# Later places for output stores in the SP queue, and one weight slice instead of two, in a fused attention and expert kernel

## The chip, the cores and the metric

The kernel runs on one core of one Trainium2 chip. The metric is the device time of one execution in microseconds. Three runs of the kernel before took 211.05, 211.3 and 212.31 us; the median is 211.3 us.

A core has five engines that run side by side, each with a queue of its own that it works off in order: TensorE (PE; weight loads are shown apart as PEld), VectorE (DVE), ScalarE (ACT), GpSimd (POOL) and SyncE (SP). They wait for one another by semaphores. Transfers are issued by an engine's queue (here SP and POOL, once ACT) and carried out by 16 DMA engines.

## The reference

A block-wise linear attention with a decay per head, whose output goes through two matrix products with a quadratic gate between them:

```python
def _attn_ref(q, k, v, lam):                  # (4, 8, 768, 64): batch, head, position, feature
    Dmask = np.where(rel >= 0, lam ** rel, 0.0)
    for b in range(nb):                        # blocks of 64 positions
        intra = np.einsum('bhic,bhjc->bhij', qb, kb) * Dmask[None]
        intra = np.einsum('bhij,bhjd->bhid', intra, vb)
        inter = np.einsum('bhid,bhde->bhie', qb * lam_pow[None], kv_state)
        out[:, :, sl] = intra + inter
        kv_state = lam_block * kv_state + np.einsum('bhsd,bhse->bhde', kb * rev_pow, vb)

def _moe_ref(x, w_in, w_out):                  # x (3072, 512), w_in (512, 2048), w_out (2048, 512)
    h = x @ w_in
    g = np.where(h >= 1, h, np.where(h <= -1, 0.0, (h + 1) ** 2 / 4))
    return g @ w_out
```

Between them the attention output is laid out as x: 4 x 768 = 3072 tokens of 8 x 64 = 512 features. Inputs and output are float32; the kernel multiplies in bfloat16.

## The kernel before, in words

**Tiling.** The 3072 tokens are cut into 24 chunks of 128 positions, six to a batch (`NCB`). The first four chunks (`NU`) are handled by a special start with units `("e", u)`. Four chunks make a stage `s` of 512 tokens for the expert part; there are six stages.

**One chunk of attention.** SP loads k, q and v of a chunk, 256 KB each (`f_load`, L426). GpSimd multiplies k and q by the decay factors and casts them to bfloat16 (L450, L453; for the first chunks VectorE casts k), and ACT casts v (L443). From chunk 6 (`XT`) a DMA transpose issued by SP (`f_tx`, L470) brings q and k into the layout for TensorE; chunks 4 and 5 are transposed on TensorE (`f_t`, L461). Then TensorE makes a "visit" `("o", c)`: the scores of the next chunk (L492, or L556 in the first chunks), the products of masked scores with v (L527, L575), the part that comes from the state (L511, L571) and the k-v products for the state two chunks ahead (L500). So a visit needs the v cast of chunk c + 2. VectorE masks the scores and sums the state, ACT copies the results into `xT`.

**The expert part.** `("l1", n)` is a group of matmuls with w_in (L606) whose result ACT passes through a ReLU (L614) and VectorE through three steps (L622, L625, L630) into `gT`. `("l2", n)` is a group of four matmuls with w_out (L639); four such groups fill one output tile `py`, which ACT copies to `osb` (L664, eight buffers, `OB`) and SP stores (`f_out`, L673, or L671 with two transfers for the tiles of the first stage). The last tile is cut in two (L649, L656, L660).

**Weights.** w_in and w_out are loaded by GpSimd's queue in ten slices (`WSL`, L146; `load_w`, L152 and L153), cast from float32 to bfloat16 on the way. An entry (0, lo, hi) is a range of blocks of 128 columns of w_in, an entry (1, lo, hi) a range of blocks of 128 rows of w_out. Three tables tie them to other work by their number in the list: the first slice waits for a load of the start (`GATE_W`, L713), slices 2 and 3 stand behind two casts of the start on GpSimd (`AFTER_W`, L714), and the load of chunk 4's k, the first of the main part, waits for slice 7 to land (`GL`, L715).

**Order of the work.** No order is written out by hand. Each piece is entered with `add(key, engine, duration, function, needs, due, ...)`, and `run_plan` (L174) works through an assumed timeline: at each step it takes the engine that comes free first and, of its ready pieces, the one with the earliest due time. The order found so is the order of the instructions in each engine's queue, and the chip keeps it whatever the real times are. `slack` is a time by which a piece is held back in the plan after its needs are met; `dma` is the assumed time of a transfer. A store `("st", y)` has due -1, so the plan puts it ahead of other ready work of SP as soon as its copy `("y", y)` is done. Stores of the first stage wait in the plan for a visit as well.

Of the kernel before, what the change touches and what calls it, by code (L numbers as in the profile page):

```python
# [23 lines left out]
def kernel(  # L24
# [19 lines left out]
    NCB = S // C  # L44
# [8 lines left out]
    NCH = n_tok // C  # L53
    CPS = MS // C
# [68 lines left out]
    for t, base in ((mask2, 0), (mask2b, 128)):  # L123
# [19 lines left out]
    w_out_sb = big.tile([128, FO, d_model], BF16)  # L143
    w_in_r = moe_w_in.rearrange("(ko ki) n -> ki ko n", ki=128)
    w_out_r = moe_w_out.rearrange("(ko ki) n -> ki ko n", ki=128)
    WSL = [(0, 0, 2), (0, 2, 4), (0, 4, 6), (0, 6, 8), (0, 8, 12), (0, 12, 16),  # L146
           (1, 0, 4), (1, 4, 8), (1, 8, 12), (1, 12, 16)]

    def load_w(i):
# [19 lines left out]
    def add(key, eng, ns, fn, needs=(), due=None, extra=0, dma=0, perf=False, mode=("full", "full"), ring=1, slack=0, late=0):  # L169
        OPS[key] = Op(key, eng, ns, fn, list(needs), due, extra, dma, perf, mode, ring, slack)  # L170
        OPS[key].late = late
        ops.append(OPS[key])
# [104 lines left out]
    def mm(*cols):  # L277
        return sum(c / 2.4 + 3 for c in cols)
# [4 lines left out]
    kq, st = {}, {}  # L283
# [382 lines left out]
    def f_out(s, ms):  # L666
        m0 = s * MS + ms * 128
        if s == 0:

            for j in range(2):  # L670
                nc.sync.dma_start(out=out[m0:m0 + 128, :].rearrange("(p j) n -> j p n", j=2)[j], in_=osb[s, ms][HD[j], :])  # L671
        else:
            nc.sync.dma_start(out=out[m0:m0 + 128, :], in_=osb[s, ms])  # L673
# [41 lines left out]
    GL = {(NU, 1): 7}  # L715
    LDMA, TSP, TDMA = 1350, 2000, 1300
    Y_TO = 9
    XSLACK, LATE, LSTEP = 400, 3000, 400


    def eng_of(name):
# [13 lines left out]
            pos_, last_ld = pos_ + 1, ("ld", c, x)  # L735
    for i in range(len(WSL)):
        add(("w", i), "POOL", 900, lambda i=i: f_w(i), [AFTER_W.get(i), ("w", i - 1) if i else None, ("ld",) + GATE_W[i] if i in GATE_W else None],
            due=i * 1e-3, dma=2650 if WSL[i][2] - WSL[i][1] == 4 else 1650)

    for u in range(NU):  # L740
        sc, r = divmod(u, 2)
# [32 lines left out]
    for c in range(NU, NCH):  # L774
        od, cb = o_due(c), c % NCB
        for x in (1, 0):
            e = "DVE" if c < XT and x == 1 else "POOL"
            add(("cast", c, x), e, 605 if e == "DVE" else 1040,
                lambda c=c, x=x, e=e: cast(c, x, eng_of(e)),
                [("ld", c, x), prev_q(c, 1, "cast") + (x,), prev_q(c, NQK, "t") + ((x,) if c - NQK < NU else ()), prev_q(c, NQK, "o") if c - NQK < NCB else ("o", c - NQK - 2), ("qT", c - NQK)], extra=90)  # L780
        add(("cast", c, 2), "ACT", 530, lambda c=c: cast(c, 2, nc.scalar),
            [("ld", c, 2), prev_q(c, NVS, "o"), prev_q(c, 1, "cast") + (2,)], extra=95)
        if c < XT:
            add(("t", c), "PE", mm(*[128] * 8), lambda c=c: f_t(c),
                [("cast", c, 0), ("cast", c, 1), ("m", c - 1, 0) if c > NU else None, ("qT", "e", NU - 1), ("kT", "e", NU - 1)],
                due=od - 6000, extra=FILL)
            add(("kT", c), "DVE", 335, lambda c=c: f_tc(c, 1), [("t", c)], extra=95)
            add(("qT", c), "DVE", 335, lambda c=c: f_tc(c, 0), [("t", c)], extra=95)
        else:
            add(("qT", c), "SP", TSP, lambda c=c: f_tx(c), [("cast", c, 0), ("cast", c, 1), prev_q(c, NQT, "o")],  # L790
                due=-2, dma=TDMA, ring=1, slack=XSLACK, late=min(LATE, LSTEP * (c - XT)))
        if c == NCB:
            add(("s", c), "PE", mm(*[64] * 12), lambda c=c: f_ahead(c),
                [("kT", c), ("qT", c), ("fc", c), ("cast", c + 1, 1), ("cast", c + 1, 2), ("f", c, 0), ("f", c, 1), ("x", c - 1), ("o", c - 1)], due=od - 3000, extra=FILL, mode=T64)
        elif c < MG:
            add(("s", c), "PE", mm(*[128] * 4), lambda c=c: f_s(c),
                [("kT", c), ("qT", c), prev_q(c, 1, "m") + (0,), prev_q(c, 1, "m") + (1,)], due=od - 3000, extra=FILL, mode=T64)
        for par in range(2):
            add(("m", c, par), "DVE", 605 if c < NCB else 340, lambda c=c, par=par: f_m(c, par),
                [("s", c) if c < MG or c == NCB else ("o", c - 1), prev_q(c, 3, "o"), ("m", c, 0) if par else ("diag",) if c == NCB else None], extra=85)  # L800
        if c < NCB:
            add(("o", c), "PE", SWITCH + mm(*[128] * 8) + (mm(*[64] * 4) if cb < NCB - 1 else 0) + (mm(*[64] * 4) if c + 1 == NCB else 0),
                lambda c=c: f_visit(c),
                [("cast", c + 1, 1), ("cast", c + 1, 2)] * (c + 1 == NCB)
                + [("m", c, 0), ("m", c, 1), ("cast", c, 2), ("cast", c, 1), ("x", c - 1), ("o", c - 1), ("kT", c), ("qT", c)]
                + ([("st", "e", NU, 0), ("st", "e", NU + 1, 0)] if c == NU else [("ub", c - 1)]),
                due=od, extra=FILL, mode=("t64", "t128"))
            if cb < NCB - 1:
                add(("ub", c), "ACT", 270, lambda c=c: f_ub(c), [("o", c)], extra=100)
            add(("x", c), "ACT", 485, lambda c=c: f_x(c), [("o", c), ("x", c - 1)], extra=105)  # L810
            continue
        for a in range(1 if cb == NCB - 1 else 2):
            add(("f", c, a), "DVE", 340, lambda c=c, a=a: f_st(c, a),
                [("s", c - 1) if c == NCB + 1 else ("o", c - 1 if c == NCB else c - 2), ("m", c - 1, 1), ("f", c, 0) if a else None if cb == 0 else ("f", c - 1, 1), ("fc", c - 2)], extra=85)
        add(("fc", c), "ACT", 485 if cb < NCB - 1 else 270, lambda c=c: f_sc(c), [("f", c, 1), ("f", c, 0), ("o", c - NUB + 1)], extra=100)
        nx = c + 1 < NCH
        add(("o", c), "PE", mm(*[64] * (6 if cb else 5)) + (mm(*[64] * 10) if nx else 0),
            lambda c=c: f_visit2(c),
            [("kT", c + 1), ("qT", c + 1), ("cast", c + 2, 1), ("cast", c + 2, 2), ("fc", c + 1), ("fc", c), ("f", c + 1, 1), ("f", c + 1, 0)] * nx
            + [("m", c, 0), ("m", c, 1), ("fc", c), ("x", c - 1), ("o", c - 1), ("s", c)] + ([("fc", c - 1)] if cb else []),  # L820
            due=od, extra=FILL, mode=("t64", "t64"))
        add(("xa", c), "ACT", 270, lambda c=c: f_xh(c, 0), [("o", c), ("x", c - 1), ("l1", (c // CPS - 2) * FO - 1)], extra=105)
        add(("x", c), "ACT", 270, lambda c=c: f_xh(c, 1), [("xa", c), ("o", c), ("x", c - 1), ("l1", (c // CPS - 2) * FO - 1)], extra=105)
# [27 lines left out]
    for n2, (_, s, ms, kg) in enumerate(l2_order):  # L851
        n = PARTS.get(s, 1)
        if s == 0:
            need = [("g", W0.index((kg, ms // 2)))]
        else:
            need = [("g", (s * FO + (ms * n // CPS) * FO // n + (4 * kg + 4) // n - 1) // RW)]
        y = s * CPS + ms
        if y == NCH - 1:
            if kg == 0:
                for part, n in ((0, CUT), (1, d_model - CUT)):  # L860
                    add(("last", part), "PE", mm(*[n] * FO), lambda part=part: f_last(part),
                        [("g", n1 // RW), ("l2", n2 - 1), ("last", 0) if part else None, ("y", y - 2 + part)],
                        due=l_due[2, s, ms, kg] + part, extra=FILL)
                    add(("y", y + part), "ACT", 400 - 240 * part, lambda part=part: f_ylast(part),
                        [("last", part), ("y", y - 1 + part), ("st", y - OB)], extra=95)
                    add(("st", y + part), "SP", 550 if s else 1100, lambda part=part: f_stlast(part), [("y", y + part), ("st", y - 1 + part)], due=-1,
                        dma=300, ring=0.2)
            continue
        need += ([("x", "e", NU - 1, 0), ("x", "e", NU - 1, 1)] + bank[True][-2:]) if y < 2 else []
        add(("l2", n2), "PE", mm(*[512] * 4), lambda a=(s, ms, kg): f_l2(*a),  # L870
            need + [w_of(1, 4 * kg), ("l2", n2 - 1), ("y", y - 2) if kg == 0 else None], due=l_due[2, s, ms, kg], extra=FILL)
        if kg == 3:
            add(("y", y), "ACT", 490, lambda a=(s, ms): f_y(*a), [("l2", n2), ("y", y - 1), ("st", y - OB)], extra=95)
            add(("st", y), "SP", 550, lambda a=(s, ms): f_out(*a), [("y", y), ("o", 9 + y)] if s == 0 else [("y", y), ("st", y - 1) if y > CPS else None], due=-1, dma=650, ring=0.2)

    run_plan({"PE": 5000, "ACT": 5000, "DVE": 5000, "POOL": 5000, "SP": 800})

# [29 lines left out]
```

## Time and profile before

| what | value |
|---|---|
| median of three runs | 211.3 us |
| profiled execution, its time | 209.96 us |
| profiled execution, its span | 208.3 us |
| instructions in the span | 6084 |
| TensorE busy | 196.9 us (95%) |
| VectorE, ACT, GpSimd busy | 130.9, 119.9, 59.1 us |
| moved by DMA | 34.47 MB, mean 166 GB/s |
| weight slices of 256 KB: number, issue to landing | 4, median 5.8 us |
| weight slices of 512 KB of w_in, of w_out | 2, 9.3 us; 4, 14.9 us |

The span runs from the first to the last instruction of the profiled execution; its time holds 1.7 us more around it. All other numbers of a profile belong to that one execution. Busy time of PE is that of matmuls, which are pipelined. L12 is line 12 of the kernel; an arrow `<-` after an idle time names what ended it. Sizes of transfers are those of the bfloat16 side.

### The profile page before, as it was taken

The numbers are of one execution on the slowest core, as the hardware profiler recorded it, in microseconds if no ns is written. First come the engines' busy times: TensorE is split into PE (matmuls) and PEld (weight loads), VectorE is DVE, ScalarE is ACT, GpSimd is POOL, SyncE is SP. The second block draws the span as 40 slices with busy tenths as digits, with TensorE's granted clock in tenths as the row PEclk, the third lists the DMA queues.
The fourth block names the chain that finished last, engine by engine and source line by source line (L and its number), as shares of the span: only waits on it lengthen the run. The fifth ranks groups of instructions, "written<-read, shape, count | busy, mean of one in ns | idle before, by whom it ended". The sixth has DMA issues, their size and how long they took to land.

```text
span 208.3 us, 6084 instructions
## 1 busy us (share of the span) xinstructions
PE 196.9 (95%) x2599; PEld 123.3 (59%) x2626; DVE 130.9 (63%) x245; ACT 119.9 (58%) x225; POOL 59.1 (28%) x72
## 2 busy tenths in 40 slices
PE   7669999999999999999999999979999999999994
PEld 2457876447966866767777777544444444444443
DVE  1475886364795983597898867942599965454000
ACT  3565773226866764875775776553788655553121
POOL 5599300135343243313344322444210000000000
PEclk9999999999999999999999999999999999999999
DMA  4999999999999999999999999999961001101212
GB/s 115 293 246 157 184 207 207 217 223 205 157 203 232 217 211 233 209 221 227 213 213 237 196 147 218 184 183 259 199 148 50 3 0 50 50 3 50 101 50 101
DMA packets 96858, 34.47 MB, mean 166 GB/s; under 512 B 82368, under 2 KB 93888, under 8 KB 96832
## 3 DMA queue, kind: packets, MB, share of 16 engines
q1 hardware_dynamic: 91408, 29.89, 71.5%
q0 software_dynamic: 5280, 4.19, 13.5%
q8 instruction: 20, 0.33, 0.7%
q14 instruction: 6, 0.05, 0.1%
q10 hardware_dynamic: 144, 0.00, 0.0%
HBM read 27.27 MB, written 6.29 MB: 161 GB/s over the span
## 4 chain that ended last, share of the span: by engine, by line
PE 73%; DMA 13%; SPq 5%; POOL 5%; issue 1%; ACT 1%; ACTq 0%
PE py L639 33%; PE ph L606 32%; DMA w_out_sb<-in_moe_w_out_dram 9%; DMA x0f<-in_q_dram 3%; SPq L470 2%; POOL w_in_sb L152 2%; SPq L302 2%; DMA x2f<-in_v_dram 2%; PE py L649 2%; PE ps L500 1%; POOL w_out_sb L153 1%; POOL qs L315 1%; PE ps L492 1%; PE po L527 1%; PE pu L527 1%
## 5 line engine op out<-in xcount | busy, mean ns | idle before, releaser
L606 PE MATMUL ph<-xT,w_in_sb 128*128 128x256 bf16 (+2 forms) x740 | 90.5, 272 | 0.2
L639 PE MATMUL py<-w_out_sb,gT 128*128 128x512 bf16 x347 | 84.5, 379 | 2.4 <-issue 1.1
L614 ACT ACTIVATE r<-ph,one 128x512 bf16<-128x512 f32 x93 | 63.4, 687 | 32.6 <-PE ph L606 28.6
L606 PEld LDWEIGHTS <-w_in_sb 128*128 128x128 bf16 x768 | 63.8, 98 | 24.1
L639 PEld LDWEIGHTS <-gT 128*128 128x128 bf16 x368 | 34.8, 98 | 37.0 <-issue 1.1
L622 DVE TENSOR_SCALAR t<-r 128x1024 bf16<-128x1024 bf16 x48 | 21.8, 454 | 27.8 <-ACT r L614 27.6
L453 POOL TENSOR_TENSOR kq<-x1f,tkd 128x512 bf16<-128x512 f32 x18 | 19.7, 1095 | 61.4 <-DMA x1f<-in_k_dram 47.8
L630 DVE TENSOR_TENSOR gT<-w,t 128x1024 bf16<-128x1024 bf16 x48 | 35.8, 745 | 1.5
L625 DVE TENSOR_TENSOR w<-r,t 128x1024 bf16<-128x1024 bf16 x48 | 33.9, 707 | 1.5
L664 ACT COPY osb<-py 128x512 f32<-128x512 f32 x23 | 13.5, 586 | 21.7 <-PE py L639 17.6
L453 POOL TENSOR_TENSOR kq<-x0f,tqd 128x512 bf16<-128x512 f32 x18 | 19.9, 1106 | 5.8 <-DMA x0f<-in_q_dram 5.7
L565 DVE TENSOR_TENSOR sd<-ps,diag 128x256 bf16<-128x256 f32 x36 | 13.6, 418 | 11.0 <-PE ps L500 10.6
L443 ACT CAST vs<-x2f 128x512 bf16<-128x512 f32 x20 | 12.3, 615 | 9.2 <-DMA x2f<-in_v_dram 8.5
L544 ACT CAST us<-st 128x512 bf16<-128x512 f32 (+1 forms) x18 | 10.4, 578 | 6.3 <-DVE st L539 6.1
L539 DVE TENSOR_TENSOR st<-st,ps 128x256 f32<-128x256 f32 x30 | 12.5, 415 | 0.6
L548 ACT CAST xT<-po 128x256 bf16<-128x256 f32 x18 | 6.8, 378 | 3.1 <-PE pu L511 2.5
L450 POOL TENSOR_TENSOR kq<-x0f,tqd 128x512 bf16<-128x512 f32 x2 | 2.1, 1040 | 20.5 <-DMA x0f<-in_q_dram 20.5
L527 PEld LDWEIGHTS <-vs 64*64 64x64 bf16 x288 | 3.7, 107 | 6.3 <-issue 5.9
L500 PE MATMUL ps<-vs,kq 64*64 64x64 bf16 x264 | 6.1, 196 | 0.9 <-ACT vs L443 0.9
L548 ACT CAST xT<-pu 128x256 bf16<-128x256 f32 x18 | 6.8, 375 | 0.3 <-PE po L511 0.3
L381 DVE TENSOR_TENSOR sc<-ps,mask 128x512 bf16<-128x512 f32 x8 | 5.2, 681 | 2.1 <-PE ps L373 2.1
L275 PE MATMUL ph<-zz 128*128 128x512 bf16 (+1 forms) x16 | 4.9, 470 | 1.3 <-DVE one L108 1.3
(87 smaller groups left out, 123.9 us busy)
## 6 DMA issues: line engine op xcount, KB each, us to landing
x0f<-in_q_dram SPq DMA_DIRECT2D x24, 256.0 KB, 5.5
x1f<-in_k_dram SPq DMA_DIRECT2D x24, 256.0 KB, 5.1
x2f<-in_v_dram SPq DMA_DIRECT2D x24, 256.0 KB, 4.6
out_dram<-osb SPq DMA_DIRECT2D x19, 256.0 KB, 2.8
w_out_sb<-in_moe_w_out_dram POOLq DMA_DIRECT2D x4, 512.0 KB, 14.9
w_in_sb<-in_moe_w_in_dram POOLq DMA_DIRECT2D x4, 256.0 KB, 5.8
w_in_sb<-in_moe_w_in_dram POOLq DMA_DIRECT2D x2, 512.0 KB, 9.3
out_dram<-osb SPq DMA_DIRECT2D x8, 128.0 KB, 4.2
```

Of the source, the lines that this page charges most:

```text
L443: (nc.scalar.copy if eng is nc.scalar else eng.tensor_copy)(t, qkv_ld[c, x])
L453: eng.tensor_tensor(t.rearrange("p (i g) d -> p g i d", g=2), qkv_ld[c, x].rearrange(h4, g=2), tb.rearrange(h4, g=2), op=AX.mult)
L539: nc.vector.tensor_tensor(st[c][:, a], st[c][:, 0] if a else st[c - 1][:, 1], kv[c][a], op=AX.add)
L548: nc.scalar.copy(out=get_xT(s)[:, :, off:off + 64], in_=po_of(c, a))
L565: nc.vector.tensor_tensor(sc_sb[c][:, par], pst[c, par], _bc(diag, 1, HP), op=AX.mult)
L606: nc.tensor.matmul(ph[:, j * m:(j + 1) * m], lhsT=w_in_sb[:, ko, (ni + j) * 128:(ni + j + 1) * 128], rhs=xT[s][:, ko, part * m:(part + 1) ...
L614: nc.scalar.activation(out=r_t[grp][:, i, :], in_=ph_t[s, ni, part], func=AF.Relu, bias=one[:, 0:1])
L622: nc.vector.tensor_scalar(t_t[grp], r, 0.5, 1.0, op0=AX.mult, op1=AX.min)
L625: nc.vector.tensor_tensor(w_t[grp], r, t_t[grp], op=AX.subtract)
L630: nc.vector.tensor_tensor(gT[s][:, f - RW * n:f, part * m:(part + 1) * m], w_t[grp].rearrange("p a (b m) -> p (a b) m", m=m), t_t[grp].rea ...
L639: nc.tensor.matmul(py_t[s, ms], lhsT=gT[s][:, ko, ms * 128:(ms + 1) * 128], rhs=w_out_sb[:, ko, :], start=(ko == 0), stop=(ko == FO - 1))
L664: nc.scalar.copy(out=osb[s, ms], in_=py_t[s, ms])
```

## The change

Four edits. The third and fourth slice of w_in become one of 512 KB, so that nine slices are left, and all later numbers in the list go down by one, while the three tables keep their numbers. Each store except those of the last stage's four tiles gets a `slack` of 3000 in the plan, which moves it back in SP's queue. The plan's assumed time of a narrow slice goes from 1650 to 1800. And a visit of the first batch that also makes the next chunk's scores is entered in the plan with the time of these matmuls and with that chunk's transposed tiles among its needs; the condition is `MG <= c + 1 < NCB`, and both constants are 6 here.

```diff
-    WSL = [(0, 0, 2), (0, 2, 4), (0, 4, 6), (0, 6, 8), (0, 8, 12), (0, 12, 16),
+    WSL = [(0, 0, 2), (0, 2, 4), (0, 4, 8), (0, 8, 12), (0, 12, 16),
            (1, 0, 4), (1, 4, 8), (1, 8, 12), (1, 12, 16)]
...
-    XSLACK, LATE, LSTEP = 400, 3000, 400
+    XSLACK, LATE, LSTEP, OSLACK = 400, 3000, 400, 3000
...
-            due=i * 1e-3, dma=2650 if WSL[i][2] - WSL[i][1] == 4 else 1650)
+            due=i * 1e-3, dma=2650 if WSL[i][2] - WSL[i][1] == 4 else 1800)
...
-            add(("o", c), "PE", SWITCH + mm(*[128] * 8) + (mm(*[64] * 4) if cb < NCB - 1 else 0) + (mm(*[64] * 4) if c + 1 == NCB else 0),
+            add(("o", c), "PE", SWITCH + mm(*[128] * 8) + (mm(*[64] * 4) if cb < NCB - 1 else 0) + (mm(*[64] * 4) if c + 1 == NCB else mm(*[128] * 4) * (c + 1 >= MG)),
                 lambda c=c: f_visit(c),
-                [("cast", c + 1, 1), ("cast", c + 1, 2)] * (c + 1 == NCB)
+                ([("cast", c + 1, 1), ("cast", c + 1, 2)] if c + 1 == NCB else [("kT", c + 1), ("qT", c + 1)] * (c + 1 >= MG))
                 + [("m", c, 0), ("m", c, 1), ("cast", c, 2), ("cast", c, 1), ("x", c - 1), ("o", c - 1), ("kT", c), ("qT", c)]
...
-            add(("st", y), "SP", 550, lambda a=(s, ms): f_out(*a), [("y", y), ("o", 9 + y)] if s == 0 else [("y", y), ("st", y - 1) if y > CPS else None], due=-1, dma=650, ring=0.2)
+            add(("st", y), "SP", 550, lambda a=(s, ms): f_out(*a), [("y", y), ("o", 9 + y)] if s == 0 else [("y", y), ("st", y - 1) if y > CPS else None], due=-1, dma=650, ring=0.2, slack=OSLACK if y < NCH - 4 else 0)
```

## The prediction

> **What bounds the kernel now.** I read the page first: the shares of busy time and the 40 slices.
>
> ```profile
> PE 196.9 (95%) x2599; PEld 123.3 (59%) x2626; DVE 130.9 (63%) x245; ACT 119.9 (58%) x225; POOL 59.1 (28%) x72
> ...
> PE   7669999999999999999999999979999999999994
> ...
> DMA  4999999999999999999999999999961001101212
> ```
>
> TensorE is busy 196.9 of 208.3 us, full from the fourth slice to the last but one, with one dent in the 27th. The DMA engines are full too, but only until about 155 us. So the end is set by TensorE's own queue, which runs in a fixed order; a transfer counts only where that queue stands waiting for it. Next, the busy time in stretches of 5 us, to see how much standing there is (columns: PE, PEld, DVE, ACT, POOL busy with counts, granted clock, DMA share, GB/s).
>
> ```profile
> core 0: us, PE busy (x) PEld busy (x) DVE busy (x) ACT busy (x) POOL busy (x), PEclk, DMA share, GB/s
> ...
> 30.00:35.00 5.00, 4.72 (x35) 3.28 (x34) 4.13 (x7) 2.10 (x4) 0.00 (x0) 1.00 1.24 205
> 35.00:40.00 5.00, 4.73 (x22) 2.11 (x22) 2.28 (x5) 0.98 (x2) 0.00 (x0) 1.00 1.14 223
> ...
> 135.00:140.00 5.00, 3.94 (x75) 2.04 (x75) 2.81 (x6) 2.18 (x6) 1.88 (x2) 1.00 1.24 185
> ```
>
> Adding all stretches, TensorE idles 5.0 us before 20 us, 2.9 us in the tail after 205, and 3.5 us between. Of these 3.5, the rows above hold 0.28 + 0.27 + 1.06 = 1.6 us. The rest are pieces of 0.05 to 0.16 us beside the attention visits, whose number does not change. So 1.6 us is the most that this change could give back.
>
> Who caused the 1.6 us is told by the timeline: the first two are waits for a w_out slice, the third for the v cast of chunk 20.
>
> ```profile
> 30.47 1.02 PE L639 MATMUL py<-w_out_sb,gT 128*128 128x512 bf16 x3 [0.23 <-DMA w_out_sb<-in_moe_w_out_dram]
> ...
> 38.65 4.48 PE L639 MATMUL py<-w_out_sb,gT 128*128 128x512 bf16 x19 [0.22 <-DMA w_out_sb<-in_moe_w_out_dram]
> ...
> 40.77 1.04 POOL L450 TENSOR_TENSOR kq<-x0f,tqd 128x512 bf16<-128x512 f32 x1 [18.25 <-DMA x0f<-in_q_dram]
> ...
> 42.96 0.61 PE L461 MATMUL po<-ident,kq 128*128 128x128 bf16 x8
> ...
> 136.13 0.62 ACT L443 CAST vs<-x2f 128x512 bf16<-128x512 f32 x1 [1.74 <-DMA x2f<-in_v_dram]
> ...
> 136.80 0.32 PE L500 MATMUL ps<-vs,kq 64*64 64x64 bf16 x16 [0.91 <-ACT vs L443]
> ```
>
> Last, SP's own waits, since the stores stand in its queue.
>
> ```profile
> SPq L673 <- ACT osb L664: 46.3, 9, 14.4
> SPq L426 <- DMA w_out_sb<-in_moe_w_out_dram: 22.2, 1, 22.2
> ...
> SPq L673 <- ACT xT L548: 1.5, 4, 0.4
> ...
> SPq L673 <- ACT r L614: 0.7, 1, 0.7
> ...
> SPq L673 <- ACT vs L443: 0.5, 1, 0.5
> ```
>
> The 46.3 us of store waits fall after 154 us, when SP has nothing else to do. The 22.2 us is the load of chunk 4's k, held until the eighth weight transfer lands. While loads are still queued behind them, stores wait only 1.5 + 0.7 + 0.5 = 2.7 us in six waits.
>
> **The change, part by part.**
>
> 1. *One weight slice for two.* GpSimd issues one transfer less (0.74 to 0.80 us each). Issue times plus time to landing put the ten slices at 17.0, 19.1, 20.4, 22.4, 25.3, 27.8, 30.4, 33.1, 35.7 and 38.6 us. Two 256 KB slices took 22.4 - 19.1 = 3.3 us; a 512 KB slice takes 2.5 to 2.9. The merged one should land at 21.6 to 22.0, and all later ones 0.4 to 0.8 us earlier. TensorE reaches its first use at 22.1 (the fifth group of L606, counted from 17.5), so a cover of 1.7 us shrinks to 0.1 to 0.5. If it lands no earlier than the fourth does now, it costs 0.3 us there, and the two waits at 30.47 and 38.65 absorb it. Those two waits go: 0 to -0.45 us, taken -0.45.
>
> 2. *The gate moves by a slice.* `GL = {(NU, 1): 7}` counts transfers, and number 7 is now the third w_out slice instead of the second. Chunk 4's k load, and the 59 loads and 18 transposes behind it on SP, leave when that lands: 35.7 - 0.4 to 0.8 = 34.9 to 35.3 instead of 33.14, later by 1.8 to 2.2. But the loads get little from leaving early now:
>
> ```profile
> q0 software_dynamic: 521, 0.52, 124.5%
> ```
>
> This is the DMA view from 33.0 to 35.5 us: only weight packets, although the k load is issued at 33.14. From 33 to 36 the hardware queue has 20 packets. Issue to first packet is thus about 2.6 us here (at the kernel's start, issue at 0.81 and no packet of that queue before 2.5: 1.7). After the change the first load packet comes at 34.9 + 1.7 = 36.6 to 35.3 + 2.6 = 37.9. Loads then land 1.1 to 1.2 us apart (39.5, 40.7, 41.8 and so on), 1.2 for the first one's own bytes and 1.3 from last byte to landing (the weights' own lag). First landing 39.1 to 40.4 against 39.5 now: the whole load stream shifts by -0.4 to +0.9, taken +0.25.
>
> The Trainium skill, "DMA: Bandwidth & Descriptors", section "Latency and other measured facts", gives about 0.6 us to the first byte of a transfer issued by SP; the section "Queues, rings and completion order" says that a DMA engine takes turns between queues that have work. By 0.6 us the loads would start before the last weight slice is done and share with it, the stream would come over 1 us earlier than now, and this part would cost nothing (sum -0.45 instead of +0.1). The 2.6 us of the trace speaks against it, so the sum goes by the trace.
>
> What waits for chunk 4: GpSimd casts its q at 40.77, the moment it lands, until 41.81. TensorE's transposes (L461) follow at 42.96. In the new order they stand one group of four L639 matmuls earlier (0.86 us in the chain: "PE py L639 x4"). With the two waits gone TensorE is there at 42.96 - 0.86 - 0.45 = 41.65, the cast is done at 41.95 + 0.25 = 42.2: a new wait of 0.55. Net at this place: 42.2 + 0.86 - 42.96 = **+0.1 us** (bounds -0.45 and +0.75).
>
> 3. *The plan moves TensorE's visits.* Neither the count nor the kind of matmuls changes, but of the 20 visits `("o", 4)` to `("o", 23)` fifteen come one group of 0.86 us earlier, one (15) two groups, four stay. Nothing is gained by that in itself; it takes cover from the loads. (The edit of a visit's planned time and needs plays no part: `MG` and `NCB` are both 6, so its condition holds for no chunk. The narrow slices' 1800 is a number in the plan alone.) Each visit needs the v cast (ACT, L443) of two chunks ahead. Cover now, start of L500 less end of the cast: chunk 8 1.6, 11 1.4, 15 1.7, 16 1.6, 17 1.4, 18 2.5, 19 0.7, 20 none (the 0.91 stall), 21 0.86, 22 0.74, 23 1.1. Nearly all hold when one group comes off, except 20 to 22.
>
> 4. *Stores behind loads.* No instruction is added or removed on SP; the 14 stores before the tail (18 transfers) move past two to five loads or transposes each. Behind each store stand all later loads and transposes, and behind these the casts on ACT and GpSimd. What can be gained is the 2.7 us of waits, and for a load that a 256 KB store now follows, the store's place in the stream, 0 to 1.2 us. In the new order this helps the v loads of chunks 11, 14, 17, 20 and 22. For 20: landing 136.1 + 0.25 - 1.2 = 135.2, cast done 135.8, visit at 135.9 with one group more left to do: 135.9 + 0.86 - 136.8 = -0.05 us at the end. For 21 no store moves ahead or behind: the visit is bound by the load at 142.0 + 0.25, cover 0.86 less one group 0.86, so +0.25, less up to 0.4 from the store wait on SP at 125.05: taken +0.1. For 22 two stores go behind, which covers its 0.1.
>
> The output buffers are no issue: with eight of them a copy needs the store eight chunks earlier, which even after the move is issued over 10 us before. After 154 us nothing changes.
>
> **Sum.** Stalls of one TensorE queue do not add, the largest shift holds: max(+0.1, -0.05, +0.1) = +0.1 us. The profiled execution took 209.96 us (span 208.3 and 1.7 around it); its time becomes 210.1. The median of the runs is 211.3, 1.3 above the profiled one, so I say **211.4 us**.
>
> **Rivals.**
>
> *All three stalls go, faster.* The loads leave the gate early enough (stream at -0.4), store places give their 1.2 us: -0.45 and nearly -0.91, 210.0 us. For it: the DMA engines are full and a store is 256 KB. Against it: the store that stood before chunk 20's v load waited for nothing there; SP was held by the transpose before it (L470 at 126.42, 4.89 us), while the DMA share fell to 0.0 to 0.3 near 129 to 130 us. The cause of the dent is therefore not a store.
>
> *Visits too early, slower.* The place is the visit of chunk 18 with the v load of chunk 20. If the stream comes at +0.9 and the moved store gives nothing, the load lands at 137.0, and one group more is left behind it: +0.9 + 0.86 = +1.76, 213.1 us. It decides once that load lands later than 136.1 - 0.86 = 135.2. ACT then stands at this cast with the ReLUs of L614 queued behind it, and TensorE has only two banks `ph` to go on with.
>
> *The change does not do what it says*, because stores hardly wait in the load phase: 0, 211.3 us, inside my forecast's band.
>
> **How the numbers follow.** Forecast, with shifts of -0.5 to +0.8: 0.62; faster rival 0.15; slower rival 0.20; something else 0.03. Unknown terms are the stream (-0.4 to +0.9), the waits (0 to -0.45) and the store places (0 to 1.2). With both rivals, the range is 209.9 (-0.45 - 0.91) to 213.1. The three runs lie 0.6% apart, so about 1% is what a measurement can tell from no change: 209.2 to 213.4. Beyond it lie only the outer ends of the rivals: faster 0.04, slower 0.10, within 0.86.
>
> **What would show it.** Step 1: no wait for w_out at 30 and 38 us; last slice at about 38. Step 2: SP's wait for w_out longer by 1.8 to 2.2 us, and a dip of the DMA share just before the first load packets; a TensorE wait before L461 of about half a microsecond. Step 3: new short waits of L500 for ACT or of L606 at visits, none over 1 us. Step 4: no store waits on SP before 150 us. I am wrong if the merged slice lands after 22.5, if the transposes on SP hold the loads for longer behind a different neighbour, or if ACT's casts, now ahead of some ReLUs, stop TensorE more than once.

## The result and the profile after

The changed kernel is slower by about one per cent. Twelve executions took 211.29 to 213.02 us, median 212.29; twelve of the kernel before beside them 208.02 to 213.06, median 211.81. The ratio of the times is 1.0107, with a 95% interval of 1.0060 to 1.0155. (A ratio leaves out, on both sides, executions that took over 1.5% longer than the fastest of the same kernel, here seven of the twelve of the kernel before and none of the changed one, so it need not equal the quotient of the medians, here 1.002.) The profiled execution took 212.27 us with a span of 210.6, against 209.96 and 208.3 before: 2.3 us more.

Where they come from is read in the idle time of TensorE's queue. After 16 us it is 5.88 us instead of 3.76. (Of 2626 matmuls each of the two traces lacks nearly the same number, 28 and 27, and these count as idle in both sums.) The stretches of 5 us show where (columns as in the prediction):

```profile
30.00:35.00 5.00, 4.95 (x37) 3.52 (x36) 4.14 (x7) 2.48 (x5) 0.00 (x0) 1.00 1.23 203
35.00:40.00 5.00, 4.95 (x24) 2.29 (x24) 2.50 (x4) 1.09 (x3) 0.42 (x1) 1.00 1.11 216
...
110.00:115.00 5.00, 3.92 (x87) 2.78 (x87) 3.62 (x8) 2.16 (x5) 1.07 (x2) 1.00 1.24 183
115.00:120.00 5.00, 4.31 (x83) 3.14 (x82) 2.59 (x4) 2.92 (x7) 1.21 (x2) 1.00 1.06 233
130.00:135.00 5.00, 4.42 (x85) 2.95 (x85) 3.97 (x7) 3.16 (x8) 2.49 (x2) 1.00 1.21 173
```

The two waits for w_out at 30 and 38 us are gone: PE 4.95 in both rows instead of 4.72 and 4.73. In their place TensorE stands five times between 104 and 150 us: 0.65 (at 104.67), 0.93 (111.46), 0.69 (118.53), 0.43 (130.86) and 0.40 (149.34), in sum 3.1 us, where the kernel before had one stall of 0.91 in the same stretch. TensorE's list of waits names what ended them (total, times, longest):

```profile
PE ps L500 <- ACT vs L443: 2.3, 3, 0.9
...
PE ph L606 <- ACT r L614: 0.8, 2, 0.4
```

Three are waits for a v cast, two for ReLUs that stand on ACT behind a v cast. (In one of these two, at 130.86, the v load had landed 0.4 us before ACT came to the cast.) The timeline of the largest, which waits for the v of chunk 16, and the SP queue ahead of it (start, duration):

```profile
103.11 3.21 SPq L470 DMA_TRANSPOSE kqT<-kq  x1
106.36 1.24 SPq L671 DMA_DIRECT2D out_dram<-osb  x2
107.64 0.59 SPq L426 DMA_DIRECT2D x2f<-in_v_dram  x1
...
111.72 0.62 ACT L443 CAST vs<-x2f 128x512 bf16<-128x512 f32 x1 [1.77 <-DMA x2f<-in_v_dram]
112.24 0.68 ACT L614 ACTIVATE r<-ph,one 128x512 bf16<-128x512 f32 x1
112.39 0.32 PE L500 MATMUL ps<-vs,kq 64*64 64x64 bf16 x16 [0.93 <-ACT vs L443]
...
112.68 1.58 SPq L673 DMA_DIRECT2D out_dram<-osb  x1
...
114.31 0.43 SPq L426 DMA_DIRECT2D x2f<-in_v_dram  x1
```

ACT stands idle for 1.77 us until the v load has landed; the ReLU behind it and TensorE's L500 follow at once. The v load was issued at 107.64, behind a store of two transfers that SP issued between the transpose and it. The last two lines show the same for the next v load, that of chunk 17: the store L673 ahead of it takes 1.58 us of SP's queue. In the kernel before, the place of chunk 16 looked like this:

```profile
103.13 2.44 SPq L470 DMA_TRANSPOSE kqT<-kq  x1
105.61 0.58 SPq L426 DMA_DIRECT2D x2f<-in_v_dram  x1
106.30 0.52 SPq L673 DMA_DIRECT2D out_dram<-osb  x1
```

There the v load leaves right behind the transpose, 2.0 us earlier than in the changed kernel, and a store follows it. Counted over the whole queue after the start: before, 5 store transfers stand directly ahead of a v load (four v loads) and 9 directly behind one; after, **16 stand directly ahead of a v load (eleven v loads) and none behind**. The waits agree. ACT's waits for v loads grow from 8.5 us in 9 waits to

```profile
ACT vs L443 <- DMA x2f<-in_v_dram: 14.3, 11, 2.9
```

and the v loads of chunks 15 to 18, whose casts the visits of 13 to 16 need, land at 104.6, 111.7, 118.5 and 124.9 us instead of 103.1, 109.2, 116.4 and 121.3, although the load stream began 1.2 us earlier (chunk 4's v landed at 40.6 instead of 41.8). Chunk 11's v still landed earlier than before (76.6 against 77.9); from chunk 12's on, ahead of which a store stands, each landed later (83.4 against 82.1). The chain of work that ended last tells the same in shares: v loads 2% before, now

```profile
PE ph L606 29%; PE py L639 27%; DMA x2f<-in_v_dram 14%; SPq L470 5%; SPq L302 4%; SPq L426 3%; PE py L649 2%; ACT r L614 2%; PE py L606 1%; ACT vs L443 1%; SPq L671 1%; POOL kq L453 1%; PE ps L500 1%; SPq L673 1%; PE pu L527 1%
```

### The profile page after: what moved, and what is told of

Its sections match the earlier page's. It is cut to its first block, busy times and chain, and to the rows that moved or that the text cites. A ratio compares the mean times of both kernels' runs of the same rounds, so it can differ in the third digit from the quotient of the medians.

```text
span 210.6 us, 6082 instructions
## 1 busy us (share of the span) xinstructions
PE 198.7 (94%) x2598; PEld 124.8 (59%) x2626; DVE 136.7 (65%) x245; ACT 119.5 (57%) x225; POOL 60.2 (29%) x71
## 4 chain that ended last, share of the span: by engine, by line
PE 64%; SPq 14%; DMA 14%; ACT 3%; issue 2%; POOL 1%
PE ph L606 29%; PE py L639 27%; DMA x2f<-in_v_dram 14%; SPq L470 5%; SPq L302 4%; SPq L426 3%; PE py L649 2%; ACT r L614 2%; PE py L606 1%; ACT vs L443 1%; SPq L671 1%; POOL kq L453 1%; PE ps L500 1%; SPq L673 1%; PE pu L527 1%
## 5 line engine op out<-in xcount | busy, mean ns | idle before, releaser
L606 PE MATMUL ph<-xT,w_in_sb 128*128 128x256 bf16 (+2 forms) x738 | 91.0, 272 | 1.0 <-ACT r L614 0.8
L606 PEld LDWEIGHTS <-w_in_sb 128*128 128x128 bf16 x768 | 64.2, 98 | 26.4 <-issue 1.6
L622 DVE TENSOR_SCALAR t<-r 128x1024 bf16<-128x1024 bf16 x48 | 25.2, 524 | 28.4 <-ACT r L614 28.3
L625 DVE TENSOR_TENSOR w<-r,t 128x1024 bf16<-128x1024 bf16 x48 | 37.4, 779 | 1.5
L453 POOL TENSOR_TENSOR kq<-x0f,tqd 128x512 bf16<-128x512 f32 x18 | 21.1, 1174 | 4.3 <-DMA x0f<-in_q_dram 4.1
L500 PE MATMUL ps<-vs,kq 64*64 64x64 bf16 x264 | 6.1, 196 | 2.4 <-ACT vs L443 2.3
L450 POOL TENSOR_TENSOR kq<-x0f,tqd 128x512 bf16<-128x512 f32 x2 | 2.5, 1240 | 19.1 <-DMA x0f<-in_q_dram 19.1
L500 PEld LDWEIGHTS <-kq 64*64 64x64 bf16 x264 | 4.9, 106 | 2.8 <-issue 2.7
```

Source lines behind the costliest of these rows:

```text
L453: eng.tensor_tensor(t.rearrange("p (i g) d -> p g i d", g=2), qkv_ld[c, x].rearrange(h4, g=2), tb.rearrange(h4, g=2), op=AX.mult)
L500: nc.tensor.matmul(kv[c][a][HD[g], i, :], lhsT=ks[c][HD[a], 2 * i + g, :], rhs=vs[c][HD[a], 4 * g + i, :], start=True, stop=True, skip_gro ...
L606: nc.tensor.matmul(ph[:, j * m:(j + 1) * m], lhsT=w_in_sb[:, ko, (ni + j) * 128:(ni + j + 1) * 128], rhs=xT[s][:, ko, part * m:(part + 1) ...
L622: nc.vector.tensor_scalar(t_t[grp], r, 0.5, 1.0, op0=AX.mult, op1=AX.min)
L625: nc.vector.tensor_tensor(w_t[grp], r, t_t[grp], op=AX.subtract)
```

## The experiments

From this three theories were formed. **P** (place): a store directly ahead of a v load delays it, and the v load is the input with the least cover. **V** (visits): the new order on TensorE and ACT has the visits and casts too early, wherever the stores stand. **W** (weights): the merged slice and the gate behind it upset the load stream. Each ratio is to the kernel before on the same chip, with 95% intervals. Where the tables below move stores, nothing else in SP's queue moves, and the other engines' orders are untouched.

### The two parts apart

Stores only (the ten slices kept):

```diff
-    WSL = [(0, 0, 2), (0, 2, 4), (0, 4, 8), (0, 8, 12), (0, 12, 16),
+    WSL = [(0, 0, 2), (0, 2, 4), (0, 4, 6), (0, 6, 8), (0, 8, 12), (0, 12, 16),
```

> The change without its weight slice: ten slices as before, only the slack of the stores. The plan then moves the stores to nearly the same places in SP's queue as the full change, and four visits one group earlier, one a group later. Theory P (place: a store now stands directly ahead of the next chunk's v load, on which ACT's cast and a TensorE visit wait): the loss of the full change is all here, +1.5 to +3 us against the kernel before, and the two waits for w_out at 30 and 38 us stay. Theory V (visits: the visits stand one group of 0.86 us earlier, ahead of their data): most visits are where they were, so at most +0.5 us. Theory W (weights: the slice and its gate upset the load stream): 0 +- 0.3 us.

Weights only (the merged slice, stores not held back; run twice):

```diff
-    XSLACK, LATE, LSTEP, OSLACK = 400, 3000, 400, 3000
+    XSLACK, LATE, LSTEP, OSLACK = 400, 3000, 400, 0
```

> The change without the stores' slack: nine slices, stores right behind their copies. The plan moves twelve visits one group earlier. Theory P: the two early waits go and nothing comes in their place, -0.3 to -0.9 us. Theory V: +1 to +2 us, with L500 waiting for ACT's v cast between 60 and 120 us. Theory W: the whole loss, +1.5 to +3 us, with the load stream later than before from chunk 4 on.

> The merged slice alone once more, as the candidate that may beat both kernels. If the 0.4 % is real the ratio to before is 0.993 to 0.999; if it was chance, 0.998 to 1.003. By either theory it is faster than the whole change by 1 % or more.

Measured: stores only 1.0065 (1.0037 to 1.0092); its queue has 16 store transfers directly ahead of ten v loads. Weights only 0.9963 (0.9925 to 1.0001) and, on another chip, 1.0043 (1.0007 to 1.0079). The two runs of the weights lie on both sides of one, so that half is no difference that was measured, and no version that beats both kernels. The loss comes with the stores (on one chip the intervals of stores only and weights only do not meet); W falls.

### The stores' place alone

The kernel before with its slices and its order on TensorE, ACT, VectorE and GpSimd; only the 14 stores stand where the change puts them:

```diff
+    ST_AT = {4: ('ld', 10, 2), 5: ('ld', 12, 2), 0: ('ld', 13, 2), 6: ('ld', 13, 2), 1: ('ld', 14, 2), 7: ('ld', 15, 0), 2: ('ld', 15, 2),
+             3: ('ld', 16, 2), 8: ('ld', 17, 2), 9: ('ld', 18, 2), 10: ('ld', 20, 2), 11: ('ld', 21, 2), 12: ('ld', 23, 0), 13: ('ld', 23, 2)}
...
-        for t, _, x in sorted(out_seq, key=lambda p: p[:2]):
+        for t, _, x in sorted(out_seq, key=...):   # store y sorts just ahead of ST_AT[y]
```

> Slices and the order on TensorE, ACT, VectorE and GpSimd exactly as before; only the 14 stores before the tail are put at the places in SP's queue that they have after the change. Theory P: +1 to +3 us, v loads of chunks 13 to 19 land 1 to 3 us later than before, and L500 waits for ACT several times. Theory V and theory W: within 0.4 us of before.

Its counterpart: the changed kernel's slices and order on the other engines, with the stores at the places of the kernel before (the same edit on the changed kernel, with this table; one transfer comes two places later, since its copy is later).

```diff
+    ST_AT = {4: ('ld', 10, 0), 5: ('ld', 11, 2), 6: ('ld', 13, 1), 0: ('ld', 13, 1), 7: ('ld', 14, 1), 1: ('ld', 14, 1), 2: ('ld', 15, 1),
+             3: ('ld', 16, 0), 8: ('ld', 17, 1), 9: ('ld', 17, 2), 10: ('ld', 20, 0), 11: ('ld', 20, 2), 12: ('ld', 22, 2), 13: ('ld', 22, 2)}
```

> Nine slices and the order on TensorE, ACT, VectorE and GpSimd exactly as after the change; the stores go back to the places in SP's queue that they had before (or as early as their copy allows). Theory P: the loss goes away, -0.5 to +0.5 us against before. Theory V: the loss stays, +1.5 to +3 us. Theory W: the loss stays too.

Measured: **1.0156 (1.0119 to 1.0192)** with only the stores moved, more than the whole change; 1.0054 (1.0015 to 1.0094) with all but the stores. So the place of the stores is enough for the whole loss. In the second kernel the v loads land about as in the kernel before (chunk 16 at 108.8 us, 109.2 there), but two waits of TensorE remain, 0.64 us for a v cast and this one for a ReLU:

```profile
147.75 1.02 PE L606 MATMUL ph<-xT,w_in_sb 128*128 128x512 bf16 x4 [1.28 <-ACT r L614]
```

### One place further back

If it is the place and not the lateness, moving the stores still later, past the v load, must bring the time back. First on the changed kernel, then on the kernel before; in both 16 of the 18 transfers stand directly behind a v load and none ahead of one. Against the table above:

```diff
-    ST_AT = {4: ('ld', 10, 2), 5: ('ld', 12, 2), 0: ('ld', 13, 2), ... 13: ('ld', 23, 2)}
+    ST_AT = {4: ('ld', 11, 1), 5: ('ld', 13, 1), 0: ('ld', 14, 1), ... 13: ('qT', 23)}
```

> The full change, with one edit: each store that stands directly ahead of a v load (12 of the 14) is put directly behind it instead, so that it is still later than in the kernel before by the same k load, q load and transpose. All other engines keep the order of the change. Theory P (place ahead of the v load): the loss goes away to what the weights alone gave, -0.8 to +0.5 us against before. Theory V (TensorE's visits and ACT's casts stand too early in the new order): +1 to +2.5 us as with the full change. A third, C (a store late in a chunk's cycle costs wherever it stands): +1 to +2.5 us.

> The kernel before with its slices and with its order on TensorE, ACT, VectorE and GpSimd. The 14 stores go back in SP's queue as far as in the run with the change's store places alone, and then past one transfer more: twelve of them stand directly behind the v load that they stood directly ahead of there. Theory P (the place directly ahead of the v load costs the time): most of the +1.6 % of that run goes, ratio to before 0.997 to 1.005, no wait of L500 or L606 over 0.8 us for a v cast. Theory L (a store moved back costs time wherever it lands, by its wait for ACT or its bytes later in the stream): +1 to +2 % as there, and waits on SP before L673 stay as long.

Measured: 0.9981 (0.9931 to 1.0031) on the changed kernel, 1.0021 (0.9984 to 1.0058) on the kernel before. The first is weak: its executions spread from 208.48 to 213.60 us (and one of 339.01), and their median, 211.96, is 0.6% above that of the kernel before, 210.67. The second is the clean pair: between its kernel and that of the run with 1.0156 only SP's queue differs, twelve stores change places with the v load next to them (the two ran on different chips, each beside the kernel before), and the medians agree with the ratios (214.02 against 210.87, and 210.54 against 210.36). What that does is seen in the queue and the waits of the two. The run with 1.0156:

```profile
109.14 1.23 SPq L671 DMA_DIRECT2D out_dram<-osb  x2
110.42 0.60 SPq L426 DMA_DIRECT2D x2f<-in_v_dram  x1
...
ACT vs L443 <- DMA x2f<-in_v_dram: 11.4, 9, 2.8
...
PE ph L606 <- ACT r L614: 4.4, 6, 1.5
...
SPq L673 <- ACT r L614: 1.9, 5, 0.6
```

and its twin, with the stores behind:

```profile
104.52 1.00 SPq L426 DMA_DIRECT2D x2f<-in_v_dram  x1
105.57 1.22 SPq L671 DMA_DIRECT2D out_dram<-osb  x2
...
ACT vs L443 <- DMA x2f<-in_v_dram: 3.9, 3, 2.8
...
PE ph L606 <- ACT r L614: 1.0, 3, 0.4
...
SPq L673 <- ACT r L614: 4.4, 4, 1.7
```

In the twin the stores wait on SP **longer** (4.4 us instead of 1.9 in the rows named after the ReLU), and it costs nothing measurable; a k load stands behind them. ACT's wait for v loads falls from 11.4 to 3.9 us. The v loads of chunks 16, 17 and 20 land at 108.2, 113.8 and 133.1 us instead of 114.6, 121.0 and 139.9. (Not all of these 6 to 7 us is the stores' doing in the first of the two: its profiled execution took 214.89 us, more than the median, and has a dip of the clock at 15 us and six holes in its load stream, both told at the end.) So neither the store's wait nor its lateness is the cause, but what is queued right behind it.

### The stores' place on the weights' order, and the whole change again

The order of the weights alone on the other engines, and SP's queue exactly that of the whole change (the weights only, with the first table above); beside it the whole change, unaltered:

> The merged slice with the order that the plan gives it (stores queued right behind their copies) on TensorE, ACT, VectorE and GpSimd; only the 14 stores stand in SP's queue where the change puts them, ahead of the v loads. Theory P: as large a loss as on the order of the kernel before, ratio to before 1.008 to 1.016, v loads of chunks 16 to 21 landing 3 to 5 us later than with the weights alone, L500 and L606 waiting for v casts. Theory V (the earlier visits and casts of the whole change's order are what costs): near the weights alone, 0.995 to 1.002.

> The whole change once more, beside the others on the same chip. Both theories: the same loss as before, ratio 1.006 to 1.015, waits of L500 and L606 of 3 us in sum; a second execution shows whether they stand at the same chunks (P and V: near chunks 16 to 21) or at others (then part of them belongs to the execution, not the kernel).

Measured: 1.0121 (1.0067 to 1.0175), as P has it and not V, though the interval just meets that of the weights alone on the same chip (1.0007 to 1.0079). P's other numbers failed in part: against the weights alone on the same chip the v loads of chunks 16, 18 and 20 land only 1.7, 1.3 and 0.6 us later (112.6, 124.9, 136.1 against 110.9, 123.6, 135.5); the 3 to 5 us had been read from an execution of the weights whose loads ran early. Nor does its profile show the waits: TensorE stood for v casts and ReLUs 1.3 us in three waits, with the weights alone 1.8 in two, and its span of 210.2 us instead of 209.0 is made in the start, by a dip of the clock. So in this row the loss is shown by the times alone. The whole change measured 1.0103 (1.0056 to 1.0150) again (medians 212.04 and 210.36), and TensorE stood at the same five places as in its first profile (0.67 at 104.45, 0.48 at 111.28, 0.28 at 117.89, 0.42 at 129.81, 0.48 at 148.28 us): these waits belong to the kernel.

All of this in one table, ratios by the order on the other engines and the place of the stores:

| order on the other engines | places of before | places of the change | behind the v load |
|---|---|---|---|
| before | 1 | 1.0156 | 1.0021 |
| weights only | 0.9963, 1.0043 (plan's own) | 1.0121 | |
| whole change | 1.0054 | 1.0107, 1.0103 | 0.9981 |

The middle column is high in each row; the step from the first column is clear of the intervals in the first row and not in the last. V is left with the 1.0054 of the last row. The 0.9981 beside it, with the same order on the other engines, would speak against it, but is weak, as said. So whether the earlier visits cost up to half a per cent stays open.

### How tight is a v load, and is the gate worth anything

In the kernel before, the v loads of chunks 9 to 22 change places with the k load behind them (stores stay behind both):

```diff
+    PUT = {('ld', c, 2): behind ('ld', c + 1, 1) for c in range(9, 23)}
```

> The kernel before, with only the v loads of chunks 9 to 22 moved: one place back, behind the k load of the next chunk (a store that stood between stays behind both). No store comes later, and nothing else moves. If the v load's place is what counts, whatever stands ahead of it (theory P): the k load's 0.6 us of issue and its 256 KB delay each v landing by 0.6 to 1.2 us, +0.7 to +2.5 us in all. If it is the stores' own doing, their waits for ACT's copy above all: within 0.4 us of before.

With the weights alone, the v loads of chunks 8 to 23 go ahead of the transposes:

```diff
+    PUT = {('ld', c, 2): ahead of ('qT', c - 1) for c in range(8, 24)}
```

> The weight slice alone (stores right behind their copies), with the v loads of chunks 8 to 23 put one place forward, ahead of the transpose that they follow. Theory P: the transpose holds SP for 2 to 5 us, so v lands 1 to 2 us earlier, no wait of L500 or of ACT for v is left, and the time is that of the weights alone or up to 1 us less: -0.3 to -1.5 us against before. If the transposes have no slack to give (they then leave 0.6 us later): 0 to +1.5 us.

Measured: 1.0037 (1.0003 to 1.0071) for one load place later, 1.0006 (0.9977 to 1.0035) for v loads earlier. A k load of the same 256 KB ahead of the v load costs a quarter of the 1.56% that the stores cost on this order. And an earlier v load gains nothing that was measured: in its profile the longest wait moves to what is now later, the transposed tiles.

```profile
106.91 0.22 PE L511 MATMUL po<-kqT,us 64*64 64x64 bf16 x2 [1.39 <-DMA kqT<-kq]
```

Last, with the weights alone, chunk 4's k load is held until the second w_out slice has landed, as in the kernel before, instead of the third:

```diff
-    lambda c=c, x=x: f_load(c, x, GL.get((c, x))),
+    lambda c=c, x=x: f_load(c, x, {(NU, 1): 6}.get((c, x))),
```

> The weight slice alone, but chunk 4's k load waits for the second w_out slice as before, not for the third; every queue's order is that of the weights alone. By the prediction's step 2 the loads leave 1.8 to 2.2 us sooner and land 0 to 0.9 us sooner; if the DMA engines are simply full with weights until they are done, no more than 0.3 us sooner, and the time is within 0.3 us of the weights alone.

Measured: 0.9985 (0.9933 to 1.0037). SP issues that k load at 32.43 us instead of 34.53, and chunk 4's v lands at 41.2 instead of 40.7: where the gate stands is worth nothing here.

## Why the prediction was wrong

I forecast 211.4 us and no measurable change, and gave a loss of over 1% a chance of 0.10. The median is 212.29, inside the range, which allows about 1% either way; but the sum held no loss beyond 0.1 us, and the cause of this one was not in it.

**One weight slice for two: right.** The merged slice landed at 21.6 us and both waits for w_out went. The gain of the later slices was too small: they landed 1.05 to 1.61 us earlier, not 0.4 to 0.8, the last at 37.0 (38 predicted).

**The gate moves by a slice: the sign was wrong.** SP's wait grew as predicted, but only by 1.4 us (22.2 to 23.6), and instead of coming 0.25 us later the load stream came 1.2 us earlier. The failed number is the 2.6 us from issue to first packet, which I read as a latency that any issue would pay. It was mostly a wait for the weight stream:

```profile
34.42 0.37 SPq L426 DMA_DIRECT2D x1f<-in_k_dram  x1
34.83 0.58 SPq L426 DMA_DIRECT2D x0f<-in_q_dram  x1
35.46 1.44 SPq L426 DMA_DIRECT2D x2f<-in_v_dram  x1
...
39.58 1.04 POOL L450 TENSOR_TENSOR kq<-x0f,tqd 128x512 bf16<-128x512 f32 x1 [16.75 <-DMA x0f<-in_q_dram]
```

The first load packet after that issue at 34.42 ran at 35.48, 1.06 us later; before it was 35.80 for an issue at 33.14, and with the earlier gate of the last experiment 35.15 for 32.43. Three issues within 2.0 us of each other start their packets within 0.65 us. Over all 14 profiles it was 2.65 to 3.28 us where two weight slices had still to land at the issue, and 1.00 to 1.06 where one had; so only about 1 us may belong to the issue itself. The loads reach full rate only when the weight stream runs out (last weight packet 38.27 before, 36.65 after), and that end moved with the merged slice. So q's cast starts at 39.58 instead of 40.77, and the new wait of 0.55 us ahead of L461 did not come. The Trainium skill, "DMA: Bandwidth & Descriptors", section "Latency and other measured facts", gives about 0.6 us to the first byte; I set it aside for the 2.6 of the trace. No run here came down to 0.6; the least was 1.00. But what it would have made of this step, a stream over 1 us earlier and no cost, is what happened.

**The plan moves TensorE's visits: the list of covers was right, the conclusion not.** I wrote that nearly all hold when one group comes off, except 20 to 22. This took the v loads to land when they do now. The covers that ran out were those of 13 to 15, because their v loads (chunks 15 to 17) came 1.5 to 2.5 us later. How much of the 3.1 us is due to the visits' own move is the open half per cent of the table.

**Stores behind loads: the step that failed.** I priced a store by its bytes in the stream, for v loads "that a 256 KB store now follows", and so found only gains, 0 to 1.2 us for chunks 11, 14, 17, 20 and 22. I did not list the loads that a store now stands directly ahead of: eleven v loads, with 16 transfers. Of the five that I named only 11 and 22 lost the store ahead of them; 17 and 20 have another there, and 14 has two transfers that it had not. Nor did I let these loads come later one after the other: the sum took the largest of three small shifts, while the v loads of chunks 15 to 18 came 1.5 to 3.6 us later. By the rows of the table, the middle column less the first, that place costs 0.5 to 1.6%, 1 to 3 us.

The traces show what the place does to a v load. In the profiles with the change's store places, with no store ahead it is issued 0.04 to 0.09 us after the transpose; with one transfer ahead 0.7 us, with two 1.2 to 1.3, with three 1.9 to 2.0, whether or not SP is seen to wait for the store's copy. Only once in the changed kernel's profile did a wait add to it (chunk 17, 1.73 us). It then lands later too: from issue to landing the v loads of chunks 12, 13, 15, 16 and 17 took 4.2 to 5.2 us in the run with 1.0156 and 3.3 to 3.7 in its twin. So the price was mostly SP's time to issue the stores and a slower landing behind them, and little of it the stores' waits. How these delays add up from chunk to chunk is not shown. A k load in the same place holds the v load for 0.6 us and costs 0.4%; that it costs less than the stores may be because two or three transfers stand ahead of the v loads of chunks 13 to 16, which was not tested by itself. The sign that I named, no store waits on SP before 150 us, was wrong as well (6.2 us in place of 2.7):

```profile
SPq L673 <- ACT r L614: 3.1, 5, 1.7
...
SPq L673 <- ACT us L544: 1.8, 2, 1.4
```

and it was the wrong sign to look for, as the twin with its 4.4 us shows.

**The rivals.** "Visits too early, slower" had the right direction and the right engine: ACT stands at a cast with ReLUs queued behind it. Its place was wrong. The v load of chunk 20 did land after my limit of 135.2 (136.7), but TensorE was late by then from the earlier stalls, and lost nothing there. "All three stalls go" was true to its name: the w_out waits went and the old stall for chunk 20 too, 1.36 us in all. The five new waits, 3.1 us, took that back and 1.7 us more.

## What to carry to other kernels

When a transfer is moved back in an in-order queue, write down two lists: what it no longer stands ahead of, and what it now stands directly ahead of, with the cover that each of those has; the second list decided here. Price each place by the time that the queue takes to issue the transfer, here 0.65 us for each, and by the later landing of the load behind it. And a delay from issue to first packet that is read while another queue fills the DMA engines need not move with the issue: here it fell from 2.65 us to 1.06 when the issue came one weight slice nearer to the end of that queue's work.

## What the runs showed that was not expected

**Holes in the load stream.** In the loading phase the DMA engines sometimes move almost nothing for 1.3 us although loads are queued. This is the DMA view of the run with 1.0156 from 142.3 to 143.5 us:

```profile
DMA packets 23, 0.01 MB, mean 5 GB/s; under 512 B 23, under 2 KB 23, under 8 KB 23
...
q1 hardware_dynamic: 23, 0.01, 4.6%
```

Counted as stretches of 0.8 us or more in which SP's transfers move less than 12 GB/s, the 14 profiles hold 36 holes between 45 and 150 us, none in that of the kernel before and up to six in others. (The number depends on these limits.) 35 of the 36 begin within 1.4 us after the start of a packet of the instruction queue (16 KB, 0.9 to 2.0 us each), of which each profile has 14 in this stretch:

```profile
q8 instruction: 20, 0.33, 0.7%
```

That is too often for chance, since such intervals cover about a fifth of the stretch; but most such packets (some 160 of 196) are followed by no hole, so what decides it is not known. Whether the holes are part of why executions of one kernel spread over 2% was not tested.

**A dip of the granted clock in the start** is in four of the 14 profiles, to half for 3.4 us:

```profile
PEclk9879999999999999999999999999999999999999
```

This is the changed kernel, on average 0.72 from 10 to 15 us. Its first L606 still starts at 17.65 us, against 17.50 before at full clock, since TensorE had idle time there. Where the dip came from 15 to 20 us, in the run with the weights' order and late stores, the first output tile was copied at 40.8 us instead of 39.6 with the weights alone on the same chip, so up to 1.2 us of a profiled time can be such a dip. It does raise the page's busy time of PE (198.7 us after, 196.9 before; from 10 to 15 us alone 4.49 against 3.41), which is therefore no sign of more work.
